# Inverse root moved ahead of relu, scaling ahead of the ELU's rest, and groups led by a piece of the second product: linear attention followed by an ELU MLP on one core

## The chip, the cores and the metric

The kernel runs on one core of one Trainium2 chip. The metric is the device time in microseconds of one execution. Before the change 16 runs gave a median of 288.81 us, from 288.42 to 291.72. The profile shown here is one further execution of 288.78 us.

## The reference

Eight batches of eight heads go through a linear attention without a mask, then each row of 64 is divided by its root mean square, and the result goes through two matrix products with an ELU between them.

```python
q, k, v: (8, 8, 576, 64);  w_in: (512, 2048);  w_out: (2048, 512)
kv  = einsum('bhsd,bhse->bhde', k, v)
o   = einsum('bhsd,bhde->bhse', q, kv)
rms = sqrt(mean(o * o, axis=-1) + 1e-6)
x   = (o / rms * g_norm).transpose(0, 2, 1, 3).reshape(4608, 512)
h   = x @ w_in
g   = where(h > 0, h, exp(min(h, 0)) - 1)
out = g @ w_out
```

## The kernel before

The 4608 rows are cut into nine groups of 512. Group T below 8 holds the first 512 rows of batch T; group 8 holds the last 64 rows of all eight batches. Each group goes through an attention with its norm, which leaves xT (the normed rows, turned) in bf16, and then through the MLP.

**The MLP of a group.** `mm1(T, i)` (line 383) is the first product: piece i, 0 to 7, makes 256 of the 2048 hidden columns in eight matmuls of 512 columns (line 399) into a PSUM tile `h_ps`, of which there are two in turn. `elu` (line 408) then lets ACT take the exponential (line 411). Its inner function `rest` puts two DVE instructions behind that: a clamp to 1 with 1 subtracted (line 420) and a combination with h into gT (line 428), which reads `h_ps` from PSUM and takes the larger of both. Where `relu` is set, ACT also writes relu(h) in bf16 (line 415), and the combination is a sum of two tiles in SBUF. The `h_ps` buffer comes free when its last reader is done: the combination, or with `relu` the two ACT instructions. `mm2(T, j, f0, f1)` (line 439) is the second product, for output rows j of four and hidden blocks f0 to f1 of sixteen: one matmul for each block (line 444), with gT as the stationary operand. When a row block j is complete, ACT copies it to SBUF (line 457), and after each second one SP issues a store (line 466).

**The norm of a group.** In `attention(T)` (line 249) the pieces are held by name. `kv` makes kv and copies it to `bd_kv`. `se0` and `se1` each make two of four row blocks of the attention output in the single PSUM tile `at` (matmuls of line 208) and let ACT square them (line 227). `sum` adds the squares by head on DVE (line 232). `inv` takes the inverse root in two small ACT instructions, Ln (line 238) and Exp (line 239). `mul` scales the rows on DVE (line 242), after which `at` may be written again. `xd` has SP issue a DMA that transposes the scaled rows (line 327), and `xg` multiplies them on DVE by g (line 334), which finishes xT. `qd` has SP issue the DMA that transposes the queries (line 265), and `landed` makes POOL wait for it (line 125), ahead of the next loads.

**The order.** The schedule is written out by hand: each engine takes its instructions in the order in which the program gives them. From T=2 on, the loop at line 774 runs the MLP's first product of group T, its second product of group T-1, and the norm of group T+1, all through `group` (line 726). Its table `start` gives each norm piece its place i: kv 0, se0 1, xd0 2, se1 3, xd1 4, xg0 5, xg1 6. A piece `se` at i brings its `sum` and `inv` in at i+1, ahead of the second product (`early`), and its `mul` at i+1 behind the ELU's rest (`late`). Each step i is then: the matmuls of `mm1`, exp and, if set, relu; the early pieces; the second product's share for i; the rest of the ELU; the late pieces. The share for i is eight blocks f of row block i // 2 of group T-1. In the pass T=2 part of group 1's second product has been done already, and six shares of four blocks each stand at i=1 to 6. In that pass relu is set for i = 1 and 2. After the loop comes the second product of group 8, with nothing beside it (line 796).

Of the kernel before, what the change touches and what calls it, by code (L numbers as in the profile page):

```python
# [16 lines left out]
def kernel(  # L17
# [362 lines left out]

    gT = {}

    def mm1(T, i, cols=(slice(0, 512),), relu=False, spare=False):

        if i == 0:
            gT[T] = mlpg.tile([P, FC, G], BF16, name="gT", tag="gT")
        x = xT[T]
        if spare:
            h_ps = [ps_m2.tile([P, G], FP32, name="h_ps", tag="mm2") for _ in range(2)]
            parts = [(a, a + 1, h_ps[a].rearrange("p (a t) -> p a t", a=1)) for a in range(2)]  # L390
        else:
            both = ps_m1.tile([P, 2, G], FP32, name="h_ps", tag="mm1")
            h_ps = [both[:, a, :] for a in range(2)]
            parts = [(0, 2, both)]
        for cs in cols:
            for a in range(2):
                f = 2 * i + a
                for c in range(KC):
                    nc.tensor.matmul(  # L399
                        h_ps[a][:, cs],  # L400
                        lhsT=w_in_sb[:, c, f * P : f * P + P],
                        rhs=x(c, cs),
                        start=(c == 0),
                        stop=(c == KC - 1),
                    )
        return elu(T, i, parts, relu)

    def elu(T, i, parts, relu):
        e = mlpt.tile([P, 2, G], BF16, name="elu_e", tag="elu_e")
        for lo, hi, ps in parts:  # L410
            nc.scalar.activation(e[:, lo:hi, :], ps, AF.Exp)  # L411
        if relu:
            h = mlpt.tile([P, 2, G], BF16, name="elu_h", tag="elu_h", bufs=2)
            for lo, hi, ps in parts:
                nc.scalar.activation(h[:, lo:hi, :], ps, AF.Relu)
            parts = [(0, 2, h)]

        def rest():
            for lo, hi, h in parts:
                nc.vector.tensor_scalar(  # L420
                    out=e[:, lo:hi, :],
                    in0=e[:, lo:hi, :],
                    scalar1=1.0,
                    scalar2=1.0,
                    op0=ALU.min,
                    op1=ALU.subtract,
                )
                nc.vector.tensor_tensor(  # L428
                    out=gT[T][:, 2 * i + lo : 2 * i + hi, :],
                    in0=e[:, lo:hi, :],  # L430
                    in1=h,
                    op=ALU.add if relu else ALU.max,
                )

        return rest
# [3 lines left out]
    def mm2(T, j, f0, f1, hold=False):  # L439

        if f0 == 0 and (T, j) not in o_ps:
            o_ps[T, j] = ps_m2.tile([P, DM], FP32, name="o_ps", tag="mm2")
        for f in range(f0, f1):
            nc.tensor.matmul(  # L444
                o_ps[T, j],
                lhsT=gT[T][:, f, j * P : j * P + P],
                rhs=w_out_sb[:, f, :],
                start=(f == 0),
                stop=(f == FC - 1),
            )  # L450
        if f1 == FC and not hold:
            mm2_out(T, j)

    def mm2_out(T, j):
        if j % 2 == 0:
            o_sb[T] = outp.tile([P, 2, DM], FP32, name="o_sb", tag="o")
        nc.scalar.copy(o_sb[T][:, j % 2, :], o_ps.pop((T, j)))  # L457
        if j % 2 == 1:
            store(T, j // 2)
# [129 lines left out]
    def scale_first(c):  # L589
# [13 lines left out]
        start=True,  # L603
# [51 lines left out]
    for c in range(KC):  # L655
        for f in (2, 3, 0, 1) if c == 0 else range(4):
# [4 lines left out]
                start=(c == 0),  # L661
                stop=(c == KC - 1),
            )
    at, ahead = attention(1), attention(2)
    for i in range(2):
        elu(0, i, [(0, 2, firsts[i])], i == 0)()
    for i in range(2, 8):
        mm1(0, i, relu=i in (2, 4, 7), spare=i in (3, 6))()
        if i in (3, 5):
            load_w_out(i // 2)  # L670
        if i == 5:
            at["q"]()
# [42 lines left out]
    def fetch(b):  # L715
        if b < B:
            fetch_packed_q(b)
            packed_kv(b)
            for name in "kv":
                fetch_packed_kv(name, b)  # L720
            unpack_q(b, Q)
        else:
            fetch_q(B)
            cast_q(B, Q)

    def group(T, at, start, second, relu=()):


        early, late = {}, {}
        for name, i in start.items():  # L730
            if name in ("se0", "se1"):
                early.setdefault(i + 1, []).extend(("sum" + name[2], "inv" + name[2]))
                late.setdefault(i + 1, []).insert(0, "mul" + name[2])
            late.setdefault(i, []).append(name)
        for i in range(9 if 8 in early else 8):
            if i == 8:
                for name in early[8] + late[8]:
                    at[name]()
                break
            rest = mm1(T, i, (slice(0, 512),), i in relu)  # L740
            for name in early.get(i, ()):
                at[name]()
            for piece in second.get(i, ()):
                mm2(*piece)
            rest()
            for name in late.get(i, ()):
                at[name]()

    ahead["landed"]()
# [1 line left out]
    at, ahead = ahead, attention(3)  # L751
    ahead["qd"]()
    for i in range(8):
        rest = mm1(1, i, relu=i in (1, 4), spare=i in (2, 5))
        rest()
        if i == 3:
            at["kv"]()
        if i == 6:
            at["se0"]()
# [13 lines left out]

    for T in range(2, NT):
        second = {i: [(T - 1, i // 2, 8 * (i % 2), 8 * (i % 2) + 8)] for i in range(8)}
        if T == 2:
            quarters = [(1, 2 + i // 4, 4 * (i % 4), 4 * (i % 4) + 4) for i in range(2, 8)]
            second = {i + 1: [piece] for i, piece in enumerate(quarters)}
        at, start = ahead, {}
        if T + 1 < NT:  # L780
            start = {"kv": 0, "se0": 1, "xd0": 2, "se1": 3, "xd1": 4, "xg0": 5, "xg1": 6}
        if T + 2 < NT:
            at["landed"]()
            fetch(T + 2)
            ahead = attention(T + 2)
        group(T, at, start, second, (1, 2) if T == 2 else ())
        if T + 2 < NT:
            ahead["qd"]()
    rows = out.rearrange("(i l s) f -> l s i f", l=2, s=S)
# [2 lines left out]
    for j, cols in pieces:  # L792
        n = cols.stop - cols.start
        ps = ps_m2.tile([P, DM], FP32, name="o_ps", tag="mm2")[:, 0:n]
        for f in range(FC):
# [4 lines left out]
                start=(f == 0),  # L800
# [36 lines left out]
```

## Time and profile before

The table is from the page of the profiled execution; its span is counted from the first to the last instruction.

| | us |
|---|---|
| median of 16 runs | 288.81 |
| the profiled execution | 288.78 |
| its span | 287.0 |
| DVE busy | 169.9 |
| ACT busy | 142.2 |
| first product (line 399), matmuls busy | 130.7 |
| second product (line 444), matmuls busy | 117.7 |
| second product of group 8 (line 796), busy | 14.0 |
| combination of the ELU (line 428), DVE busy | 77.5 |
| exp of the ELU (line 411), ACT busy | 73.0 |

A row of a timeline has the start in us, the length in us, the engine, the line, the operation with what it writes and reads, the shape, how many instructions are merged, and in brackets how long the engine had been idle before it and what it waited for. Matmuls are pipelined and their ends are modelled: one of 512 columns shows 379 ns, while the next starts sooner than that. PE is TensorE's matmuls, PEld its loads of the stationary operand.

In the chain of work that ended last, the passes begin with the first product of their piece 0 at these times: T=3 at 95.20 us, T=4 at 124.71, T=5 at 154.15, T=6 at 183.49, T=7 at 212.93, T=8 at 241.90.

### The profile page before, as it was taken

The numbers are of one execution on the slowest core, as the hardware profiler recorded it, in microseconds if no ns is written. First come the engines' busy times: TensorE is split into PE (matmuls) and PEld (weight loads), VectorE is DVE, ScalarE is ACT, GpSimd is POOL, SyncE is SP. The second block draws the span as 40 slices with busy tenths as digits, with TensorE's granted clock in tenths as the row PEclk, the third lists the DMA queues.
The fourth block names the chain that finished last, engine by engine and source line by source line (L and its number), as shares of the span: only waits on it lengthen the run. The fifth ranks groups of instructions, "written<-read, shape, count | busy, mean of one in ns | idle before, by whom it ended". The sixth has DMA issues, their size and how long they took to land.

```text
span 287.0 us, 4829 instructions
## 1 busy us (share of the span) xinstructions
PE 276.1 (96%) x1971; PEld 133.6 (47%) x2001; DVE 169.9 (59%) x220; ACT 142.2 (50%) x204; POOL 53.4 (19%) x94
## 2 busy tenths in 40 slices
PE   6899899999999899999999999999999999999994
PEld 2445454445544444444444544454444444444444
DVE  5459461778388758755865587557755775444400
ACT  2779544785485455336533554345444544443211
POOL 7835302431421241004210421011000000000000
PEclk9999999999999999999999999999999999999999
DMA  7999999796995598145953499255614230010122
GB/s 195 204 206 203 206 204 160 223 171 129 165 176 58 147 167 181 37 128 87 192 127 97 79 188 172 73 131 115 122 47 102 70 79 33 40 64 11 73 73 73
DMA packets 55961, 35.96 MB, mean 125 GB/s; under 512 B 32772, under 2 KB 53508, under 8 KB 55940
## 3 DMA queue, kind: packets, MB, share of 16 engines
q0 software_dynamic: 20192, 17.30, 38.9%
q1 hardware_dynamic: 35348, 17.83, 24.7%
q10 hardware_dynamic: 400, 0.52, 0.5%
q8 instruction: 15, 0.25, 0.4%
q14 instruction: 6, 0.05, 0.1%
HBM read 36.70 MB, written 9.44 MB: 161 GB/s over the span
## 4 chain that ended last, share of the span: by engine, by line
PE 85%; DMA 10%; DVE 1%; issue 1%; ACT 1%; DVEq 0%; POOLq 0%
PE h_ps L399 38%; PE o_ps L444 37%; DMA w_out_sb<-in_moe_w_out_dram 6%; PE o_ps L796 5%; DMA w_in_sb<-in_moe_w_in_dram 3%; PE at L208 2%; DMA k_pk<-in_k_dram 2%; PE at L177 2%; ACT elu_e L411 1%; PE at L306 0%; DVE xs L242 0%; DVE gT L428 0%; PE at L217 0%; PE se_ps L208 0%; DVE elu_e L420 0%
## 5 line engine op out<-in xcount | busy, mean ns | idle before, releaser
L399 PE MATMUL h_ps<-xT,w_in_sb 128*128 128x512 bf16 x555 | 130.7, 379 | 1.0 <-DVE xT L334 0.7
L444 PE MATMUL o_ps<-w_out_sb,gT 128*128 128x512 bf16 x490 | 117.7, 379 | 1.3 <-DMA w_out_sb<-in_moe_w_out_dram 0.2
L411 ACT ACTIVATE elu_e<-h_ps 128x1024 bf16<-128x1024 f32 (+1 forms) x75 | 73.0, 982 | 86.2 <-PE h_ps L399 84.6
L399 PEld LDWEIGHTS <-w_in_sb 128*128 128x128 bf16 x560 | 53.5, 98 | 62.9 <-DVE xT L334 1.2
L428 DVE TENSOR_TENSOR gT<-elu_e,h_ps 128x1024 bf16<-128x1024 bf16 (+1 forms) x67 | 77.5, 1157 | 7.0
L444 PEld LDWEIGHTS <-gT 128*128 128x128 bf16 x512 | 49.8, 98 | 59.4 <-DMA w_out_sb<-in_moe_w_out_dram 0.3
L420 DVE TENSOR_SCALAR elu_e<-elu_e 128x1024 bf16<-128x1024 bf16 (+1 forms) x76 | 33.2, 437 | 70.7 <-ACT elu_e L411 70.6
L457 ACT COPY o_sb<-o_ps 128x512 f32<-128x512 f32 x32 | 18.5, 586 | 21.0 <-PE o_ps L444 21.0
L232 DVE TENSOR_REDUCE ss<-sq 128x16 f32<-128x1024 bf16 x16 | 19.3, 1218 | 8.4 <-ACT sq L227 8.4
L151 POOL COPY q_bf<-q_pk 128x512 bf16<-128x512 bf16 x24 | 14.6, 636 | 29.2 <-DMA q_pk<-in_q_dram 29.2
L242 DVE TENSOR_TENSOR xs<-at,ss 128x1024 bf16<-128x1024 f32 x14 | 17.0, 1217 | 0.0
L227 ACT ACTIVATE sq<-at 128x1024 bf16<-128x1024 f32 x14 | 14.4, 1027 | 1.4 <-PE at L208 1.4
L796 PE MATMUL o_ps<-w_out_sb,gT 128*128 128x512 bf16 (+1 forms) x79 | 14.0, 336 | 0.1
L125 POOL COPY gate<-qT 1x1 bf16<-1x1 bf16 x6 | 1.2, 203 | 65.0 <-DMA qT<-q_bf 65.0
L104 POOL DMA_DIRECT2D q_pk<-in_q_dram x14 | 10.6, 762 | 3.0 <-issue 1.8
L796 PEld LDWEIGHTS <-gT 128*128 128x128 bf16 x80 | 7.8, 98 | 6.2
L356 ACT CAST bd_kv<-at 64x256 bf16<-64x256 f32 (+1 forms) x16 | 5.4, 338 | 8.5 <-PE at L177 8.4
L118 POOL DMA_DIRECT2D k_pk<-in_k_dram x12 | 8.4, 698 | 5.6 <-DMA w_in_sb<-in_moe_w_in_dram 2.6
L208 PEld LDWEIGHTS <-qT 128*128 128x128 bf16 x112 | 7.3, 98 | 4.1 <-issue 1.2
L118 POOL DMA_DIRECT2D v_pk<-in_v_dram x12 | 8.5, 711 | 2.2 <-DMA w_in_sb<-in_moe_w_in_dram 1.8
L177 PEld LDWEIGHTS <-k_pk 64*64 64x64 bf16 x576 | 6.6, 107 | 3.8 <-issue 3.6
L208 PE MATMUL at<-bd_kv,qT 128*128 128x128 bf16 x96 | 7.3, 219 | 1.1 <-ACT bd_kv L356 0.6
(71 smaller groups left out, 113.6 us busy)
## 6 DMA issues: line engine op xcount, KB each, us to landing
out_dram<-o_sb SPq DMA_DIRECT2D x16, 512.0 KB, 3.0
q_pk<-in_q_dram POOLq DMA_DIRECT2D x14, 256.0 KB, 5.8
k_pk<-in_k_dram POOLq DMA_DIRECT2D x6, 576.0 KB, 8.3
v_pk<-in_v_dram POOLq DMA_DIRECT2D x6, 576.0 KB, 11.0
w_in_sb<-in_moe_w_in_dram POOLq DMA_DIRECT2D x4, 512.0 KB, 10.9
w_out_sb<-in_moe_w_out_dram POOLq DMA_DIRECT2D x4, 512.0 KB, 14.8
st_q<-in_q_dram SPq DMA_DIRECT2D x2, 512.0 KB, 4.9
st_q<-in_q_dram SPq DMA_DIRECT2D x16, 64.0 KB, 2.7
```

Of the source, the lines that this page charges most:

```text
L118: nc.gpsimd.dma_start(out=raw[name, b].rearrange("p h j d -> p h (j d)")[:, hs], in_=in_[:, hs])
L151: eng.tensor_copy(out=out_, in_=in_)
L208: nc.tensor.matmul(ov[:, u, :, s, :], lhsT=qT(p, j), rhs=bd_kv[:, T, p, :], start=True, stop=True,)
L232: nc.vector.reduce_sum(out=ss, in_=sq.rearrange("p c (h e) -> p (c h) e", h=H), axis=AX.X)
L242: nc.vector.tensor_tensor(out=xs.rearrange("p c (h e) -> p (c h) e", h=H), in0=se_ps.rearrange("p c (h e) -> p (c h) e", h=H), in1=ss.to_b ...
L399: nc.tensor.matmul(h_ps[a][:, cs], lhsT=w_in_sb[:, c, f * P : f * P + P], rhs=x(c, cs), start=(c == 0), stop=(c == KC - 1),)
L411: nc.scalar.activation(e[:, lo:hi, :], ps, AF.Exp)
L420: nc.vector.tensor_scalar(out=e[:, lo:hi, :], in0=e[:, lo:hi, :], scalar1=1.0, scalar2=1.0, op0=ALU.min, op1=ALU.subtract,)
L428: nc.vector.tensor_tensor(out=gT[T][:, 2 * i + lo : 2 * i + hi, :], in0=e[:, lo:hi, :], in1=h, op=ALU.add if relu else ALU.max,)
L444: nc.tensor.matmul(o_ps[T, j], lhsT=gT[T][:, f, j * P : j * P + P], rhs=w_out_sb[:, f, :], start=(f == 0), stop=(f == FC - 1),)
L457: nc.scalar.copy(o_sb[T][:, j % 2, :], o_ps.pop((T, j)))
L796: nc.tensor.matmul(ps, lhsT=gT[B][:, f, j * P : j * P + P], rhs=w_out_sb[:, f, cols], start=(f == 0), stop=(f == FC - 1),)
```

## The change

There are three parts.

- The early pieces (`sum`, `inv`) now go to `elu` and come between exp and relu, where they came behind both. That makes a difference only where relu is set.
- In a step with relu set, a late piece `mul0` or `mul1` now goes ahead of the ELU's rest. In T=2 relu is set at i=4 as well. So in that pass both halves of group 3's norm have their inverse root ahead of relu, and their scaling ahead of clamp and combination.
- In passes from T=3 on, the first share of the second product (eight blocks of row block 0 of group T-1) is put ahead of the pass, before its first matmuls of `mm1`. The other seven shares move from i to i-1, and i=7 has none.

```diff
-    def mm1(T, i, cols=(slice(0, 512),), relu=False, spare=False):
+    def mm1(T, i, cols=(slice(0, 512),), relu=False, spare=False, between=()):
...
-        return elu(T, i, parts, relu)
-
-    def elu(T, i, parts, relu):
+        return elu(T, i, parts, relu, between)
+
+    def elu(T, i, parts, relu, between=()):
         e = mlpt.tile([P, 2, G], BF16, name="elu_e", tag="elu_e")
         for lo, hi, ps in parts:
             nc.scalar.activation(e[:, lo:hi, :], ps, AF.Exp)
+        for piece in between:
+            piece()
         if relu:
...
-            rest = mm1(T, i, (slice(0, 512),), i in relu)
-            for name in early.get(i, ()):
-                at[name]()
+            rest = mm1(
+                T, i, (slice(0, 512),), i in relu, between=[at[name] for name in early.get(i, ())]
+            )
             for piece in second.get(i, ()):
                 mm2(*piece)
+            names = late.get(i, [])
+            if i in relu and names[:1] in (["mul0"], ["mul1"]):
+                at[names.pop(0)]()
             rest()
-            for name in late.get(i, ()):
+            for name in names:
                 at[name]()
...
         second = {i: [(T - 1, i // 2, 8 * (i % 2), 8 * (i % 2) + 8)] for i in range(8)}
-        if T == 2:
+        if T > 2:
+            mm2(*second[0][0])
+            second = {i - 1: second[i] for i in range(1, 8)}
+        else:
             quarters = [(1, 2 + i // 4, 4 * (i % 4), 4 * (i % 4) + 4) for i in range(2, 8)]
             second = {i + 1: [piece] for i, piece in enumerate(quarters)}
...
-        group(T, at, start, second, (1, 2) if T == 2 else ())
+        group(T, at, start, second, (1, 2, 4) if T == 2 else ())
```

## The prediction

> **What bounds the kernel now.** I read the page's busy times first, then TensorE's own waits, then the timelines of TensorE, DVE and ACT around the two waits that lie in the stretch of the change, and last the same timelines at the end of the run.
>
> ```profile
> span 287.0 us, 4829 instructions
> PE 276.1 (96%) x1971; PEld 133.6 (47%) x2001; DVE 169.9 (59%) x220; ACT 142.2 (50%) x204; POOL 53.4 (19%) x94
> ...
> PEclk9999999999999999999999999999999999999999
> ```
>
> TensorE is busy for 96% of the span at full granted clock; nothing else passes 60%. So the kernel can only gain where TensorE waits. Eight products with 512 columns start 1.73 us apart from the next eight, 0.216 us each, and this rhythm runs on without a break in the groups from 3 on. Of TensorE's own waits, two belong to the second half of the run:
>
> ```profile
> PE h_ps L399 <- DVE xT L334: 0.7, 1, 0.7
> PE at L208 <- DVE xs L242: 0.4, 1, 0.4
> ```
>
> Their places, in TensorE's timeline (start, length, and in brackets idle time and releaser):
>
> ```profile
> 82.93 1.03 PE L444 MATMUL o_ps<-w_out_sb,gT 128*128 128x512 bf16 x4
> 84.39 0.61 PE L208 MATMUL at<-bd_kv,qT 128*128 128x128 bf16 x8 [0.43 <-DVE xs L242]
> ...
> 92.61 1.89 PE L399 MATMUL h_ps<-xT,w_in_sb 128*128 128x512 bf16 x8
> 95.20 1.90 PE L399 MATMUL h_ps<-xT,w_in_sb 128*128 128x512 bf16 x8 [0.71 <-DVE xT L334]
> ```
>
> Both are in loop pass T=2, where the norm of group 3 is made, and at its seam to T=3. Idle time undercounts them, since a matmul's shown end lies after the start of the next. From start to start: four products from 82.93 should hand over at 82.93 + 4 x 0.216 = 83.80, but the next starts at 84.39: 0.59 lost. Eight from 92.61 should hand over at 94.34, next starts 95.20: 0.86 lost. Together 1.45 us, the most that this change can give. Why DVE is late, in its timeline:
>
> ```profile
> 80.39 1.22 DVE L232 TENSOR_REDUCE ss<-sq 128x16 f32<-128x1024 bf16 x1 [0.22 <-ACT sq L227]
> 81.60 0.43 DVE L420 TENSOR_SCALAR elu_e<-elu_e 128x1024 bf16<-128x1024 bf16 x1
> 82.52 0.69 DVE L428 TENSOR_TENSOR gT<-elu_e,elu_h 128x1024 bf16<-128x1024 bf16 x1 [0.48 <-ACT elu_h L415]
> 83.12 1.22 DVE L242 TENSOR_TENSOR xs<-at,ss 128x1024 bf16<-128x1024 f32 x1
> ...
> 91.16 1.22 DVE L428 TENSOR_TENSOR gT<-elu_e,h_ps 128x1024 bf16<-128x1024 bf16 x1
> ...
> 94.67 0.48 DVE L334 TENSOR_SCALAR xT<-xT,g_col 128x1024 bf16<-128x1024 bf16 x1
> ```
>
> The scaling at 83.12 stands behind an ELU combination that itself waited for ACT's relu, and the inverse root stood behind that relu too:
>
> ```profile
> 81.47 1.02 ACT L415 ACTIVATE elu_h<-h_ps 128x1024 bf16<-128x1024 f32 x1
> 82.37 0.31 ACT L238 ACTIVATE ss<-ss,eps_col 128x16 f32<-128x16 f32 x1
> 82.71 0.22 ACT L239 ACTIVATE ss<-ss 128x16 f32<-128x16 f32 x1
> ```
>
> **Part 1: the reorder at i=2.** Exp of piece 2 ends at 81.57 and the sum at 81.61, so Ln can start at 81.66 and its Exp at 82.00, end 82.22. The scaling runs from about 82.25 to 83.47 in place of 84.34, ahead of the 83.80 at which TensorE wants the tile. All 0.59 us go. Price: relu runs 82.12 to 83.14, the output copy behind it on ACT moves from 82.83 to 83.04, and Exp of piece 3 from 83.30 to 83.50. DVE's rest of piece 2 starts at 83.38, and that of piece 3 at 84.56 (before 84.36), its combination ending at 86.31 (before 86.11). TensorE needs that buffer for piece 5 at 87.43 - 0.59 = 86.84: hidden, with 0.5 us to spare.
>
> **Part 2: i=4, with a relu added.** The second sum starts at 86.29 and ends at 87.51; Ln, Exp, then scaling 88.14 to 89.36, where it ran from 89.51 before. So the second transpose is issued 1.4 us sooner. DVE idles 0.6 us for it (87.51 to 88.14), and the rest of piece 4 waits behind it: clamp 89.27, combination 89.80; rest of piece 5: clamp 90.40, combination 90.93 to 92.15. Piece 7 takes piece 5's buffer and is due at 92.61 - 0.59 = 92.02; released at about 92.20 it waits 0.18 us. This is the first thing late next. Its bounds: 0 if the scaling gets going 0.2 us sooner, 0.6 if DVE's order costs another 0.4. Relu 4 on ACT, 88.01 to 89.03, frees its buffer before piece 6 is due at 89.43. The Trainium skill (ScalarE: Activation LUTs, Rules for kernel authors) speaks against the added relu: it gives relu and max to VectorE, up to three times faster in bf16. The rows by form say what it buys here: DVE's combination takes 1.221 us reading h_ps from PSUM and 0.692 us reading a relu made on ACT, for 1.02 us on ACT, half of which is idle. Following the rule, piece 5's combination would end 0.53 later and piece 7 would wait 0.7 in place of 0.18. The row decides here, since the waiting engine is DVE.
>
> **Part 3: a leading piece from T=3 on.** The work is moved, not added: the same second products, each piece one place sooner. At the seam T=2/3, TensorE has eight products (1.73 us) after piece 7. The last scaling of xT ends near 94.66 on my walk and the first product of group 3 is then due at 92.20 + 2 x 1.73 = 95.66: no wait. The position 'lead and first piece done' comes at 97.39 against 95.20 + 3.45 = 98.65 before: 1.27 us gained, which is 0.59 + 0.86 - 0.18. In later groups the rhythm 'eight and eight' stays. The leading piece reads gT's first half only, finished four pieces earlier. The piece behind it reads gT's last two columns about 4.8 us after the first product ended, where the chain exp, clamp, combination takes 3.0: hidden by 1.8 us.
>
> What moves along: the output copies and stores. On SP the first store now stands ahead of the first transpose of xs in place of behind it; the second comes before the end of the group, and the qT transpose behind it is free about 3.4 us sooner, with the loads that wait for its landing on POOL. The first transpose has far to go: in T=5 it is issued at 168.09, and DVE takes its result at 177.86. Nothing, as long as it lands in that time; see the rivals.
>
> **Part 4: the end.** After the last first-product piece, eight second products used to run ahead of the closing ones. They are gone from there:
>
> ```profile
> 267.64 1.89 PE L444 MATMUL o_ps<-w_out_sb,gT 128*128 128x512 bf16 x8
> ...
> 269.15 3.77 PEld L796 LDWEIGHTS <-gT 128*128 128x128 bf16 x18
> 269.37 3.83 PE L796 MATMUL o_ps<-w_out_sb,gT 128*128 128x512 bf16 x17
> 269.43 1.22 DVE L428 TENSOR_TENSOR gT<-elu_e,h_ps 128x1024 bf16<-128x1024 bf16 x1
> ```
>
> The closing products now follow the last first-product piece at once, as the eight did at 267.64. On the clock of these lines the fifteenth, which reads gT's last columns, is then due at 267.64 + 14 x 0.216 = 270.66. gT is ready at 270.65. The skill (TensorE: Matmul & The Clock Gate, Step-by-step: what each phase is for) says weight loads are pulled ahead of running matmuls and so hidden; by that alone this costs nothing. The rows show loads 0.22 us ahead of their matmuls (269.15 to 269.37), so this one, due at 270.44, must wait. Where a load waited in the head of the run, its matmul started at once after it. I take 0.1, bounds 0.05 to 0.25.
>
> **Sum.** 0.59 + 0.86 - 0.18 - 0.10 = 1.17 us. The profiled execution took 288.78 (span 287.0), within 0.03 of the median 288.81, so 287.6 either way. A difference of about 0.2% (0.58 us, that is, 288.23) is what a measurement of this kernel can tell from no change.
>
> **Rivals.** *A wait takes the place of those removed (0.15), 288.3.* The scaling ahead of the ELU leaves DVE idle twice for 0.6 us; if ACT's chain is slower than I walked, piece 7 waits 0.6 and the end 0.25: 1.45 - 0.85 = 0.6 gained. For it: the slack at piece 7 is already negative. Against: relu 4 takes 0.53 off DVE.
>
> *Earlier loads collide, nothing is gained (0.08), 288.8.* POOL's casts of q follow the loads, 3.4 us sooner against the products, and DVE's clamp took 0.83 to 0.88 us in place of 0.43 beside such a cast. The first scaling of group 4's norm ends at 109.66 and TensorE wants its tile at 110.29: one collision is already in that row and a second of 0.45 is covered by the 0.63 between; a third would leave TensorE waiting 0.3, and in each of the four groups 3 to 6 that returns 1.2 us.
>
> *Slower: the transposes behind the stores (0.09), 290.4.* Store and transpose share SP's queue. In T=5 the transpose landed after 8.3 us and the store, then behind it, after 7.7. Beyond 9.8 us DVE waits; then come 1.06 us of its own idle time (before its clamp at 179.40) and 2.1 us of buffer slack (its combination ends at 181.15, TensorE wants that buffer at about 183.3), so TensorE stalls from a landing at about 13 us. Were the store's 7.7 to count in full, 8.3 + 7.7 - 1.7 head start = 14.3: a 1.4 us stall; the kernel gets slower where this happens in two groups of the four with loads (2.8 - 1.2 = +1.6 us, or 290.4), and where it averages 0.3 us in each the gain is gone. Against: the usual landing is 3.0 to 3.3, and the loads move away from the transposes.
>
> **Numbers.** The likeliest (0.68) gives 287.6, its own range 287.3 to 288.1. It lies below 288.23 whole; with 0.06 of the first rival that is 0.74 for faster. Same: 0.09 of the first rival and the second, 0.17. Slower: the third, 0.09. The range 287.3 to 288.5 leaves out the third rival, most of the second and little of the first and the low edge: under 0.2.
>
> **What would show it.** In the profile after: no wait at L208 for xs; the first scaling starting 0.7 us after the exp of piece 2 ends; a wait of 0 to 0.6 us at a first-product piece for gT (L428) near 92; no wait for xT at the seam; at the end a weight load waiting for gT near 271 and a TensorE wait of at most 0.25; xs transposes landing below 9 us in T=3 to 7. I would be wrong if TensorE's waits for gT or for xT in groups 3 to 8 come to more than 0.3 us in all, or if the wait at piece 7 is above 0.6.

## The result, and the profile after

Nine runs of the changed kernel gave a median of 287.34 us (287.29 to 287.59), where the runs of the kernel before, now 48, have 288.73. The ratio is 0.9951 with a 95% interval of 0.9938 to 0.9963: 1.4 us faster (1.1 to 1.8). The forecast was 287.6. The profiled execution took 287.37, against 288.78.

TensorE's waits in the whole run; the two for xs and for xT are gone, and all that is left lies ahead of T=2:

```profile
PE bank L196 <- DVE q_bf L151: 1.3, 1, 1.3
PE bank L527 <- DVE zeros L502: 1.2, 1, 1.2
PE at L208 <- ACT bd_kv L356: 0.6, 1, 0.6
PE o_ps L446 <- DMA w_out_sb<-in_moe_w_out_dram: 0.4, 1, 0.4
PE bank L583 <- ACT sq L577: 0.4, 1, 0.4
PE bank L567 <- DVE kv L561: 0.3, 1, 0.3
PE kv_ps L177 <- issue: 0.3, 1, 0.3
```

TensorE's timeline of the same stretch. This pass begins at 73.11, 0.07 later than before:

```profile
83.00 1.03 PE L446 MATMUL o_ps<-w_out_sb,gT 128*128 128x512 bf16 x4
83.86 0.61 PE L208 MATMUL at<-bd_kv,qT 128*128 128x128 bf16 x8
...
91.21 1.03 PE L446 MATMUL o_ps<-w_out_sb,gT 128*128 128x512 bf16 x4
92.25 1.89 PE L399 MATMUL h_ps<-xT,w_in_sb 128*128 128x512 bf16 x8
93.98 1.67 PE L446 MATMUL o_ps<-w_out_sb,gT 128*128 128x512 bf16 x7
95.70 1.89 PE L399 MATMUL h_ps<-xT,w_in_sb 128*128 128x512 bf16 x8
```

The first pair hands over after 0.86 us, so no wait. The second takes 1.04 for four products, 0.18 too much. The list of waits above doesn't show this one, since the modelled ends of the four hide it; only the starts do. Then eight and eight follow each other in 1.73 and 1.72 us: the seam has no wait. DVE and ACT show where the 0.18 come from:

```profile
79.54 1.08 DVE L430 TENSOR_TENSOR gT<-elu_e,elu_h 128x1024 bf16<-128x1024 bf16 x1 [0.49 <-ACT elu_h L417]
...
82.37 1.23 DVE L242 TENSOR_TENSOR xs<-at,ss 128x1024 bf16<-128x1024 f32 x1 [0.62 <-ACT ss L239]
...
88.19 1.22 DVE L242 TENSOR_TENSOR xs<-at,ss 128x1024 bf16<-128x1024 f32 x1 [0.62 <-ACT ss L239]
...
89.85 0.69 DVE L430 TENSOR_TENSOR gT<-elu_e,elu_h 128x1024 bf16<-128x1024 bf16 x1
...
90.98 1.22 DVE L430 TENSOR_TENSOR gT<-elu_e,h_ps 128x1024 bf16<-128x1024 bf16 x1
...
94.17 0.48 DVE L334 TENSOR_SCALAR xT<-xT,g_col 128x1024 bf16<-128x1024 bf16 x1
```

```profile
87.94 0.22 ACT L239 ACTIVATE ss<-ss 128x16 f32<-128x16 f32 x1
88.06 1.01 ACT L417 ACTIVATE elu_h<-h_ps 128x1024 bf16<-128x1024 f32 x1
```

DVE idles 0.62 us ahead of each scaling for the inverse root. The combination of piece 5 (90.98) ends at 92.20, and piece 7, which writes into its buffer, starts 0.05 later. The size of this wait differs between executions. In a second one of the changed kernel, whose pass begins at 72.93, it is 0.97 - 0.86 = 0.11 us; the combination of piece 1, the first with relu in the pass, took 0.82 us there (from 79.36) in place of the 1.08 above (from 79.54), and the `sum` behind it started 7.35 us into the pass (80.28) in place of 7.43 (80.54). Its rows at piece 7:

```profile
91.04 1.03 PE L446 MATMUL o_ps<-w_out_sb,gT 128*128 128x512 bf16 x4
92.01 1.89 PE L399 MATMUL h_ps<-xT,w_in_sb 128*128 128x512 bf16 x8
```

At the end of the run the load of the fifteenth stationary operand waits for gT, as these rows of TensorE's loads show:

```profile
267.69 2.90 PEld L804 LDWEIGHTS <-gT 128*128 128x128 bf16 x14
270.97 10.73 PEld L804 LDWEIGHTS <-gT 128*128 128x128 bf16 x66 [0.37 <-DVE gT L430]
```

What it costs is read from the first copy of a closing block on ACT, here after and then before the change:

```profile
271.61 0.59 ACT L812 COPY o_last<-o_ps 128x512 f32<-128x512 f32 x1 [2.48 <-PE o_ps L804]
```

```profile
273.02 0.59 ACT L804 COPY o_last<-o_ps 128x512 f32<-128x512 f32 x1 [2.87 <-PE o_ps L796]
```

It starts 3.70 us after the first closing product (267.91 to 271.61) and did so after 3.65 before (269.37 to 273.02): 0.05 us. In the experiments below it is 3.70 or 3.71 wherever the last group has a leading piece, and 3.65 or 3.66 wherever it has none.

### The profile page after: what moved, and what is told of

Read it like the earlier page. It is cut to its first block, busy times and chain, and to the rows that moved or that the text cites. A ratio compares the mean times of both kernels' runs of the same rounds, so it can differ in the third digit from the quotient of the medians.

```text
span 285.6 us, 4829 instructions
## 1 busy us (share of the span) xinstructions
PE 275.6 (97%) x1971; PEld 133.5 (47%) x2001; DVE 168.7 (59%) x220; ACT 144.0 (50%) x205; POOL 53.1 (19%) x94
## 4 chain that ended last, share of the span: by engine, by line
PE 87%; DMA 10%; issue 1%; ACT 1%; DVE 0%; POOLq 0%
PE h_ps L399 39%; PE o_ps L446 38%; DMA w_out_sb<-in_moe_w_out_dram 6%; PE o_ps L804 5%; DMA w_in_sb<-in_moe_w_in_dram 3%; DMA k_pk<-in_k_dram 2%; PE at L208 2%; PE at L177 2%; PE at L306 0%; PE at L217 0%; ACT elu_e L411 0%; PE se_ps L208 0%; ACT bd_kv L356 0%; PE xt_ps L306 0%; DVE elu_e L422 0%
## 5 line engine op out<-in xcount | busy, mean ns | idle before, releaser
L430 DVE TENSOR_TENSOR gT<-elu_e,h_ps 128x1024 bf16<-128x1024 bf16 (+1 forms) x66 | 76.3, 1156 | 6.9
L422 DVE TENSOR_SCALAR elu_e<-elu_e 128x1024 bf16<-128x1024 bf16 (+1 forms) x76 | 32.4, 427 | 71.0 <-ACT elu_e L411 71.0
L417 ACT ACTIVATE elu_h<-h_ps 128x1024 bf16<-128x1024 f32 x9 | 9.2, 1019 | 0.0
L208 PEld LDWEIGHTS <-qT 128*128 128x128 bf16 x112 | 7.3, 98 | 3.5 <-issue 0.5
L430 DVE TENSOR_TENSOR gT<-elu_e,elu_h 128x1024 bf16<-128x1024 bf16 x9 | 6.6, 735 | 2.9 <-ACT elu_h L417 2.4
```

Of the source, the lines that this page charges most:

```text
L422: nc.vector.tensor_scalar(out=e[:, lo:hi, :], in0=e[:, lo:hi, :], scalar1=1.0, scalar2=1.0, op0=ALU.min, op1=ALU.subtract,)
L430: nc.vector.tensor_tensor(out=gT[T][:, 2 * i + lo : 2 * i + hi, :], in0=e[:, lo:hi, :], in1=h, op=ALU.add if relu else ALU.max,)
```

## The experiments

The profiled executions differ by up to 2 us before the pass T=2 begins (in four of the experiments the granted clock is 0.7 in the second of the 40 slices, ahead of anything that was edited). So beside the medians I compare the stretch from the first product of T=2 to the end of the last copy on ACT. One more thing varies there from one execution to the next: the 72 small products of `kv` take 0.71 us in most passes and 0.82 to 0.85 in T=4 or T=6 of some. The last column, the corrected stretch, takes that excess out. Each row is one profiled execution; the three kernels that have two rows agree in the last column within 0.01 to 0.06 us, so a smaller difference there shows nothing.

| kernel | median us | stretch us | kv excess | without it |
|---|---|---|---|---|
| before | 288.73 | 210.75 | 0.22 | 210.53 |
| after | 287.34 | 209.27 | 0 | 209.27 |
| lead alone | 287.79 | 209.84 | 0.13 | 209.71 |
| norm alone | 288.15 | 210.19 | 0.25 | 209.94 |
| inverse root early, scaling not | 288.64 | 210.66 | 0.13 | 210.53 |
| scaling early, inverse root not | 288.19 | 210.24 | 0.14 | 210.10 |
| no relu at i=4 | 288.76 | 210.80 | 0.13 | 210.67 |
| relu at i=5 too | 287.11 | 209.25 | 0.13 | 209.12 |
| lead at T=3 alone | 287.15 | 209.26 | 0 | 209.26 |
| relu at i=5, lead at T=3 alone | 287.13 | 209.20 | 0.12 | 209.08 |
| after, again | 287.33 | 209.34 | 0.13 | 209.21 |
| step i=4 as before | 287.29 | 209.34 | 0.12 | 209.22 |
| relu at i=5 too, again | 287.25 | 209.23 | 0.13 | 209.10 |
| both, again | 287.11 | 209.07 | 0 | 209.07 |

The theory on trial is that of the prediction: single waits of TensorE in T=2 and at its seam, set by DVE's order and by when an `h_ps` buffer comes free. The main rivals: the gain comes from the shifted shares in later groups, or from one half of the reorder alone.

**The leading pieces alone.** The norm's pieces and relu in T=2 as before the change.

```diff
-            rest = mm1(
-                T, i, (slice(0, 512),), i in relu, between=[at[name] for name in early.get(i, ())]
-            )
+            rest = mm1(T, i, (slice(0, 512),), i in relu)
+            for name in early.get(i, ()):
+                at[name]()
...
-            if i in relu and names[:1] in (["mul0"], ["mul1"]):
-                at[names.pop(0)]()
...
-        group(T, at, start, second, (1, 2, 4) if T == 2 else ())
+        group(T, at, start, second, (1, 2) if T == 2 else ())
```

> The leading piece alone, the norm of group 3 ordered as before. Theory (the waits are single, and each part takes away its own): the wait for xs at L208 stays (0.59 us from start to start), piece 7 finds its buffer free, the wait for xT is gone: 0.18 less 0.59 against the changed kernel, so 287.34 + 0.41 = 287.75. Rival (the leading piece brings more by the shifted shares and the earlier loads in groups 4 to 8, some 0.2 us): then also 287.75, but the groups after T=3 are shorter than before in this profile too. Rival (the lead only works if the norm is early): xT is still waited for, 288.2 or above.

Measured: 287.79, ratio 0.9962 (0.9942 to 0.9982). The wait for xs is there (0.4 in the list of waits, 0.60 from start to start), the one for xT is not. So the lead makes 0.82 of the 1.26 us by the corrected stretch, with a late norm too, and the last rival falls.

**The norm alone.** The shares of the second product as before the change.

```diff
-        if T > 2:
-            mm2(*second[0][0])
-            second = {i - 1: second[i] for i in range(1, 8)}
-        else:
+        if T == 2:
```

> The norm's reorder with relu at i=4, without the leading piece. Theory: no wait at L208, 0.18 us for gT's buffer at piece 7, and then the first product of group 3 waits for xT until about 94.7 on the clock of the kernel before, where it started at 95.20: 0.49 gained, 288.73 - 0.49 = 288.24. Rival (what the norm gains early is all handed on to the end of the pass): 287.9 or below.

Measured: 288.15, ratio 0.9985 (0.9969 to 1.0001), so alone it can't be told from no change by its ratio. In the profile the corrected stretch is 0.59 shorter: the wait at L208 is gone, and group 3's first product starts 21.57 us after the pass T=2 began, against 22.16. It still waits for xT: 0.6 us in the list of waits, 94.61 - 92.12 - 1.73 = 0.76 from start to start. Neither half of the change gives the whole, and 0.82 + 0.59 is 0.15 more than 1.26: piece 7's wait comes with the norm and shows in full once the seam no longer hides it.

**Inverse root early, scaling not.**

```diff
-            if i in relu and names[:1] in (["mul0"], ["mul1"]):
-                at[names.pop(0)]()
```

> The changed kernel with the scaling put back behind the ELU's rest; the inverse root stays ahead of relu. Theory (DVE's order decides): the ELU's combination now waits for a relu that comes 0.7 us later, and the scaling behind it ends at about 85.0 in place of 83.5, so TensorE waits 1.2 us at L208, more than the 0.59 before the change; about 0.1 at piece 7: 287.34 + 1.15 = 288.5. Rival (the early inverse root is what helps, the place of the scaling matters little): within 0.2 of 287.34.

Measured: 288.64, ratio 1.0 (0.9984 to 1.0016): the whole gain is lost. TensorE's and then DVE's rows:

```profile
82.78 1.03 PE L446 MATMUL o_ps<-w_out_sb,gT 128*128 128x512 bf16 x4
84.95 0.62 PE L208 MATMUL at<-bd_kv,qT 128*128 128x128 bf16 x8 [1.14 <-DVE xs L242]
```

```profile
83.07 0.69 DVE L430 TENSOR_TENSOR gT<-elu_e,elu_h 128x1024 bf16<-128x1024 bf16 x1 [1.19 <-ACT elu_h L417]
83.68 1.22 DVE L242 TENSOR_TENSOR xs<-at,ss 128x1024 bf16<-128x1024 f32 x1
```

From start to start 2.17 us where four products take 0.86: a wait of 1.31. The inverse root was ready in time, but DVE stood 1.19 us at the combination for the relu that now came later, with the scaling behind it.

**Scaling early, inverse root not.**

```diff
-            rest = mm1(
-                T, i, (slice(0, 512),), i in relu, between=[at[name] for name in early.get(i, ())]
-            )
+            rest = mm1(T, i, (slice(0, 512),), i in relu)
+            for name in early.get(i, ()):
+                at[name]()
```

> The changed kernel with the inverse root put back behind relu; the scaling stays ahead of the ELU's rest. Theory: the scaling starts when the inverse root is done, at 82.98, hardly sooner than before the change (83.12), and holds up the rest behind it: 0.45 us wait at L208 and 0.67 at piece 7, in place of 0 and 0.18: 287.34 + 0.94 = 288.3. Rival (the scaling's place is what helps, the inverse root's place matters little): within 0.2 of 287.34.

Measured: 288.19, ratio 0.9992 (0.998 to 1.0005), a stretch 0.83 longer than the changed kernel's. DVE waits 1.27 us for the inverse root ahead of the first scaling and 0.99 ahead of the second. TensorE then waits at L208 (84.82 - 83.52 - 0.86 = 0.44) and at piece 7 (93.60 - 92.17 - 0.86 = 0.57). Both moves are needed at i=2: with one of them alone the kernel has a longer corrected stretch (210.53 and 210.10) than with the lead and neither (209.71).

**No relu at i=4.**

```diff
-            if i in relu and names[:1] in (["mul0"], ["mul1"]):
+            if T == 2 and i in (2, 4) and names[:1] in (["mul0"], ["mul1"]):
...
-        group(T, at, start, second, (1, 2, 4) if T == 2 else ())
+        group(T, at, start, second, (1, 2) if T == 2 else ())
```

> The changed kernel without relu at i=4 (both halves still have inverse root and scaling ahead). Theory: the combination of piece 4 reads PSUM again and takes 1.22 in place of 0.69 us, piece 5's ends 0.53 later, and piece 7 waits 0.7 in place of 0.18: 287.34 + 0.53 = 287.87. Rival (ACT's 1.02 us for the relu holds up piece 5's exp as much as it relieves DVE): 287.34 or less.

Measured: 288.76, ratio 1.0005 (0.9986 to 1.0025): 1.4 us lost, not 0.53. The loss is not at piece 7, where the theory put it: piece 5's combination does end 0.46 us later in the pass, but piece 7 starts 0.86 us behind its four products and doesn't wait. The theory overlooked piece 6. TensorE's rows:

```profile
88.47 1.03 PE L446 MATMUL o_ps<-w_out_sb,gT 128*128 128x512 bf16 x4
90.89 1.89 PE L399 MATMUL h_ps<-xT,w_in_sb 128*128 128x512 bf16 x8 [1.40 <-DVE gT L430]
```

and DVE's:

```profile
87.96 1.22 DVE L242 TENSOR_TENSOR xs<-at,ss 128x1024 bf16<-128x1024 f32 x1 [0.62 <-ACT ss L239]
...
89.62 1.22 DVE L430 TENSOR_TENSOR gT<-elu_e,h_ps 128x1024 bf16<-128x1024 bf16 x1
```

Without relu, piece 4's buffer is held until its combination ends at 90.84, behind the scaling, and piece 6 wants it at 89.33: 1.56 us. In the changed kernel relu freed it at 89.07 (88.06 + 1.01), and piece 6 started at 89.49. What the relu buys is the early release: 1.4 us, nearly three times the 0.53 us that it takes off DVE.

**Relu at i=5 too**, run twice, the second time beside the changed kernel in one set of runs.

```diff
-        group(T, at, start, second, (1, 2, 4) if T == 2 else ())
+        group(T, at, start, second, (1, 2, 4, 5) if T == 2 else ())
```

> The changed kernel with relu at i=5 as well. Theory: piece 5's buffer comes free with relu (about 90.9) in place of the combination (92.2), piece 7 doesn't wait: 287.34 - 0.18 = 287.16. Rival (the wait at piece 7 is for something else, or the added relu delays piece 6's exp): 287.34 or more.

> Relu at i=5 as well, once more, in one set with the changed kernel. Theory: 0.18 less than it. Rival (no difference, its first run was low with its set): within 0.05 of it.

Measured: 287.11 and 287.25; the changed kernel beside the second 287.33. Piece 7 starts 0.87 us behind the four products ahead of it: its wait is gone. The corrected stretch is 0.15 and 0.17 shorter than in the first execution of the changed kernel, where piece 7 waited 0.18, and 0.09 and 0.11 shorter than in the second, where it waited 0.11. The medians put the gain at 0.08 in one set, too near to their scatter to prove it.

**The lead at T=3 alone, without and with relu at i=5**, the latter twice.

```diff
-        if T > 2:
+        if T == 3:
             mm2(*second[0][0])
             second = {i - 1: second[i] for i in range(1, 8)}
-        else:
+        if T == 2:
```

> The leading piece at T=3 alone; from T=4 on the second product's shares stand as before the change. Theory: the lead does its work at one seam, and the last group gets its cover of eight products back, so the 0.05 us at the end go: 287.29. Rival (0.2 us of the gain come from the shifted shares in groups 4 to 8, by earlier stores and loads): 287.5.

> Both: relu at i=5 as well, and the leading piece at T=3 alone. Theory: 0.18 and 0.05 add: 287.34 - 0.23 = 287.1, with TensorE waiting nowhere from T=2 on. Rival: the two don't add, 287.3 or more.

> Relu at i=5 and the leading piece at T=3 alone, once more, in one set with the changed kernel. Theory: 0.23 less than it. Rival: within 0.05 of it.

Measured: 287.15 alone; 287.13 and 287.11 with relu at i=5. With the lead at one seam only, nothing is lost (209.26 against 209.27 and 209.21), so the shifted shares, stores and loads of groups 4 to 8 gave nothing that can be seen. The profiles of before and after say the same: from the first product of group 3 to the handover behind group 8's last one TensorE does the same work in 172.22 us before (95.20 to 267.64, less 0.22 of `kv` excess) and in 172.21 after (95.70 to 267.91). The closing copy comes 3.66 us after the first closing product again, 0.04 less. Both edits together are the fastest by the corrected stretch, 0.13 to 0.20 us below the changed kernel, with no wait of TensorE in the list from T=2 on. In one set the medians say 287.11 against 287.33, ratios to the kernel before of 0.995 (0.9935 to 0.9965) and 0.9953 (0.9941 to 0.9965), which overlap: by the medians the gain is not shown.

**Step i=4 as before**, beside the changed kernel once more.

```diff
-        group(T, at, start, second, (1, 2, 4) if T == 2 else ())
+        group(T, at, start, second, (1, 2) if T == 2 else ())
```

> The changed kernel itself, beside the next three, so that their differences of 0.1 to 0.2 us are read in one set. Every theory: 287.34, within 0.15.

> The changed kernel with step i=4 left as before the change: no relu there, the second half's scaling behind the ELU's rest; the first half's reorder at i=2 and the leading pieces stay. Theory (at i=4 relu and the scaling ahead only pay for each other: the relu frees piece 4's buffer, which the scaling ahead would hold up): piece 4's combination ends at 89.2, ahead of piece 6 at 89.4; piece 5's ends at 92.0, and piece 7 waits 0 to 0.05; xT is 0.1 us earlier than in the changed kernel and under the leading piece: 0.18 less than the changed kernel, 287.16. Rival (the second half's early scaling is needed for xT, or relu at i=4 is needed anyway): 287.5 or above.

Measured: 287.29, and 287.33 for the changed kernel. The rival falls: under the lead, the second half's earlier scaling and the relu that makes it affordable bring nothing. The 0.18 that I expected to gain is not there either: the corrected stretch is 209.22, against 209.21 for the changed kernel in the same set, and piece 7 waits 0.11 us in both. I had put its wait at 0 to 0.05; DVE's clamp took 0.60 us and the combination followed late:

```profile
87.42 0.60 DVE L422 TENSOR_SCALAR elu_e<-elu_e 128x1024 bf16<-128x1024 bf16 x1
88.13 1.22 DVE L430 TENSOR_TENSOR gT<-elu_e,h_ps 128x1024 bf16<-128x1024 bf16 x1
```

## Why the prediction was right, step by step

- *The wait at L208, 0.59:* gone in full, by both moves at i=2 together; either alone leaves 0.44 or 1.31.
- *The wait at piece 7, 0.18:* 0.18 in the profiled execution and 0.11 in the second, from the release that was named. Relu at i=5 takes it away. That the first agrees so well is in part luck: I had counted on from a `sum` that starts 7.35 us into the pass, as before the change. The second execution had that start and waited 0.11; the first started at 7.43, behind a combination that took 1.08 us in place of 0.69.
- *The seam, 0.86:* gone in full, by the lead. The lead alone does it.
- *The end, 0.10:* measured 0.05, the lower bound. The pulled-ahead load waited 0.37 us, as the rows of before let expect, and nearly all of that lay under the products ahead of it: gT was ready at 270.91, the load started at 270.97, and its product was due at 267.91 + 14 x 0.216 = 270.93. The result lies midway between my 0.10 and the 0 that the rule of the Trainium skill (TensorE: Matmul & The Clock Gate, Step-by-step: what each phase is for) gives alone.
- *The sum, 1.17:* 1.26 in the corrected stretch, and 1.32 with the second execution of the changed kernel. Of the 0.09 beyond the forecast, 0.05 are the end; in the second execution 0.07 more are the wait at piece 7. The remaining 0.03 to 0.04 are less than executions of one kernel differ by. The two profiled executions differ by 1.41: these 1.26 and the 0.22 of `kv` excess before, less 0.07 by which the one of after came later to the pass T=2. How much of such excess is in the medians, 1.39 apart, is not known, and why those products take 0.11 to 0.14 longer in some executions stays open.
- *The rivals:* the wait in place of the others came to 0.23 in all, not 0.85. The collisions between POOL's casts and DVE's clamp did not reach TensorE in groups 3 to 8, which took 172.2 us before and after. The transposes behind the stores did not get slower: the eight of twelve with a landing on record took 3.0 to 4.3 us, where one of before took 8.3, and DVE's list of waits from T=2 on has none for a transpose. In T=5 the store ahead was issued 1.7 us sooner than the transpose, and the loads 4.7 us sooner than before (157.15 against 161.87).
- *A size was wrong:* the query transpose at the end of a pass is issued 3.0 us sooner (122.83 against 125.79 at the end of T=3). Of that 1.3 is what the whole pass runs ahead, so 1.7 are its own, one place of eight products, not the 3.4 that I put. Nothing hung on it.
- *One step was wrong:* the weighing of the relu at i=4 against the rule of the Trainium skill (ScalarE: Activation LUTs, Rules for kernel authors). I put following the rule at 0.53 us, at piece 7 alone. The price is 1.4 us while the scaling stands ahead of the ELU's rest, since piece 4's buffer is then released 1.5 us late for piece 6; and about nothing when the scaling goes behind as well (287.29 against 287.33). It was a side sum and not part of the 1.17. The early scaling of the second half, which sends the transpose off 1.4 us sooner, was worth nothing under the lead.

## What to carry to other kernels

When one engine is busy throughout, list its single waits from start to start, not by idle time, and ask of each who holds the tile or buffer back; here two waits were 1.45 us, and the change gave 1.26 of them. A step pulled ahead in one queue pushes what it passes, and what it passes may hold a buffer: two moves that each lose alone can win together, as the inverse root and the scaling did here. Cover at a seam (eight products here) can make finer reordering ahead of it needless, as it did for step i=4.

## What the runs showed of the hardware that was not expected

- DVE's clamp, 0.43 us, took 0.92 us with the scaling put back and 0.60 in the last experiment. POOL cast a part of q at the same time in both (84.84 to 85.44 beside the clamp from 84.81; 87.14 to 87.74 beside the clamp from 87.42). Over the fourteen profiles, from the pass T=2 on, the 678 clamps with no POOL instruction beside them took 0.41 to 0.43 us; of the 106 with one beside them, 39 took 0.47 to 0.92. The combination that reads a relu from SBUF took 0.69 in all 27 cases alone and 0.82 to 1.08 in 9 of 15 beside POOL; the one that reads PSUM took 1.22 in all 742. No run moved POOL's work by itself, so that it is the cause is not shown.
- A wait of 0.18 us of TensorE is not in its list of waits, as 379 ns are shown for a product and the next starts after 216; waits of 0.59, 0.86, 1.31 and 1.56 are shown as 0.43, 0.71, 1.14 and 1.40, each 0.15 to 0.17 too short, about the 0.16 between 379 and 216 ns.
